# Token tiles of v, with their ones column, at a stride of 192 bytes instead of 130

## The chip, the cores and the metric

The kernel runs on one core of one Trainium2 chip. The metric is the device time of one execution in microseconds (us).

## The reference

Sparse attention (4 batches, 8 heads, 768 tokens, head dimension 64) followed by a gated feed-forward layer:

```python
scores = scale * np.matmul(q, k.transpose(0, 1, 3, 2))
scores = np.where(mask, scores, -1000000000.0)
attn = np.exp(scores - np.max(scores, axis=-1, keepdims=True))
attn = attn / (np.sum(attn, axis=-1, keepdims=True) + 1e-09)
o = np.matmul(attn, v)
# ... o is laid out as x: 3072 tokens x 512
gate = 1.0 / (1.0 + np.exp(-(x @ w_gate)))
out = (gate * (x @ w_val)) @ w_out
```

The argument touches only `attn @ v` and the row sum of `attn`.

## The kernel before

The tokens are cut into six tiles of 128. For each head and token tile, v stands in SBUF as 64 columns in fp16, followed by one column of ones. One matmul thus gives both the product and, in column 65, the sum that divides it. The layout is dense: 65 elements of 2 bytes, so a tile begins 130 bytes after the one before.

```python
vex = [sing.tile([128, H, NT, D + 1], f16, name=f"vex{r}") for r in range(2)]
for r in range(2):
    nc.vector.memset(vex[r][:, :, :, D : D + 1], 1.0)
# ...
def go(eng):                                  # VectorE: v of one batch and two heads
    nc.vector.tensor_copy(
        vex[b % 2][:, 2 * p : 2 * p + 2, :, 0:D],
        v16[:, 2 * p : 2 * p + 2, :, :],
    )
# ...
def pv(self, s):                              # TensorE: called with s = 0 and s = 1
    acc = spare[self.bank.slot][:, 0 : 4 * (D + 1)]
    self.acc = acc.rearrange("a (s h d) -> a s h d", s=2, h=2)
    for a in range(2):
        for t in range(NT):
            nc.tensor.matmul(
                self.acc[:, s, a, :],
                self.steps[t // 2].pt[:, a, t % 2, s * 128 : (s + 1) * 128],
                vex[self.b % 2][:, 2 * self.p + a, t, :],
                start=(t == 0),
                stop=(t == NT - 1),
            )
```

The two calls make 24 matmuls in a row: twice (s) over two heads (a) and six token tiles (t). There are 48 such groups, 1152 matmuls. Each has a weight load of its own (the probabilities, 128 columns), and v is the operand that streams: the profile of before lists 1152 loads of `pt`, 128x128, and 1152 matmuls with 128x65 of `vex`. The order of all work comes from a planner with fixed costs, so it does not depend on the layout.

The softmax here doesn't subtract the row's maximum and nothing guards it: scores larger than these inputs give would overflow.

Of the kernel before, what the change touches and what calls it, by code (L numbers as in the profile page):

```python
# [13 lines left out]
f16 = mybir.dt.float16  # L14
# [6 lines left out]
B, H, S, D = 4, 8, 768, 64  # L21
BLK = 32
NB = S // BLK
NT = S // 128
# [10 lines left out]
XB, PB, VB = 4, 5, 5  # L35
BIG = 1024.0
FFN_LAG = 3



# [83 lines left out]
def kernel(  # L124
# [18 lines left out]
            name=nc.get_next_instruction_name(), act_func_set_id=_set_id  # L143
# [17 lines left out]
    sing = ctx.enter_context(tc.tile_pool(name="sing", bufs=1))  # L161
# [17 lines left out]
    qp = sing.tile([128, NP, NT, 2, D], f16, name="qp")  # L179
    kp = sing.tile([128, NP, NT, 2, D], f16, name="kp")  # L180
    v16 = sing.tile([128, H, NT, D], f16)
    vex = [sing.tile([128, H, NT, D + 1], f16, name=f"vex{r}") for r in range(2)]
    qT = [sing.tile([128, NP, S], f16, name=f"qT{r}") for r in range(2)]
    kT = [sing.tile([128, NP, S], f16, name=f"kT{r}") for r in range(2)]

# [296 lines left out]
    class Pair:  # L482
# [9 lines left out]
        def pv(self, s):  # L492
# [4 lines that stand above are left out]
                    nc.tensor.matmul(  # L497
                        self.acc[:, s, a, :],
                        self.steps[t // 2].pt[:, a, t % 2, s * 128 : (s + 1) * 128],
                        vex[self.b % 2][:, 2 * self.p + a, t, :],  # L500
                        start=(t == 0),
                        stop=(t == NT - 1),
                    )
# [66 lines left out]
    def scores(run):  # L570


        def mm(eng):
            for pr, st in run:
                st.qk()

        deps = [
            x for pr, st in run for x in kdone[pr.b, pr.p] + qdone[pr.b, pr.p, pr.u]
        ]
        first = run[0][0].n == 0  # L580
        if first:
            deps.append(t_bias)
        a = plan.add(
            [(PE, 0.1 + (0.44 if first else 0.22) * len(run))],
            mm,
            deps,
            take=[st.bank for pr, st in run],
        )
        for pr, st in run:
            read["qk", pr.b, pr.p] = [a]  # L590
            i = NP * pr.n + pr.p - VB
            old = [used["P"][i]] if i >= 0 else []
            e = plan.add([(ACT, 0.98)], st.exp, [a] + old, free=[st.bank])
            if first:
                pr.products.append(e)
                continue
            pr.products.append(plan.add([(DVE, 0.66)], st.mul, [e] + masks[st.j, st.u]))
# [239 lines left out]
    for n in range(1, len(units)):  # L837
# [5 lines left out]
        for sl in range(6):  # L843
# [4 lines left out]
            else:  # L848
                scores(run)
            part = parts.popleft() if n > 1 or sl >= FFN_LAG else []  # L850
            for i, fn in enumerate(part):
# [50 lines left out]
```

## Time and profile before

| | before |
|---|---|
| time, median (range of runs) | 298.56 us (298.49 to 298.87) |
| span of the profiled run | 297.6 us (that run took 299.34 us) |
| TensorE busy | 289.9 us, 97% |
| ScalarE, VectorE busy | 205.1 us, 191.0 us |
| value product (line 497) | 1152 matmuls; 0.77 us on the chain for 24 |

The prediction shows the lines themselves. Below, the *distance* of two matmuls is the time from the start of one to the start of the next. It is read from the pieces of the chain (duration divided by count) or from the records' start times, never from the mean duration of one matmul (at line 497 that is 194 ns, while one starts every 32 ns). The *chain* is the sequence of work that ended last, followed back from the end.

### The profile page before, as it was taken

What the parts mean: (1) busy time and instruction counts of PE and PEld (TensorE: products, weight loads), DVE (VectorE), ACT (ScalarE), POOL (GpSimd) and SP (SyncE); (2) the same over time, 40 slices, a digit from 0 to 9 for tenths busy, and PEclk for the clock granted to TensorE, in tenths of its full rate; (3) what the DMA queues carried; (4) which work ended last, traced back from release to release, by engine and by line L of the source; (5) the groups of instructions that cost most, each with busy time, mean ns of one, the idle gap of its engine ahead of it and who ended that gap; (6) DMA issues with size and microseconds to landing.
All of it is one profiled execution on the core that took longest, in us unless ns stands there. A gap on an engine that the chain in (4) does not pass through costs nothing.

```text
span 297.6 us, 7862 instructions
## 1 busy us (share of the span) xinstructions
PE 289.9 (97%) x3302; PEld 206.2 (69%) x3302; DVE 191.0 (64%) x439; ACT 205.1 (69%) x323; POOL 48.5 (16%) x65
## 2 busy tenths in 40 slices
PE   7998999999999999999999999999999999999994
PEld 2655785786786786786776786686687687687771
DVE  3588877875675677676576577577477477475240
ACT  2689977677677677677777776777777677672331
POOL 8944100197000000097100000000000000000000
PEclk9999999999999999999999999999999999999999
DMA  7999999999900200999940202920201200201101
GB/s 109 185 201 203 206 204 205 212 174 149 193 12 9 90 13 10 173 177 133 179 70 18 83 11 56 203 64 20 79 11 20 79 11 20 78 15 20 70 2 71
DMA packets 74540, 28.55 MB, mean 96 GB/s; under 512 B 57352, under 2 KB 71560, under 8 KB 74504
## 3 DMA queue, kind: packets, MB, share of 16 engines
q0 software_dynamic: 40400, 14.16, 43.7%
q1 hardware_dynamic: 33924, 13.75, 20.5%
q8 instruction: 26, 0.43, 0.6%
q10 hardware_dynamic: 180, 0.13, 0.1%
q14 instruction: 10, 0.08, 0.1%
HBM read 28.55 MB, written 6.29 MB: 117 GB/s over the span
## 4 chain that ended last, share of the span: by engine, by line
PE 92%; ACT 2%; DMA 2%; DVE 1%; POOL 1%; issue 0%; ACTq 0%; POOLq 0%
PE m L617 44%; PE m L657 22%; PE s L459 12%; PE m L497 12%; DMA k<-in_k_dram 2%; ACT pt L469 2%; PE s L451 1%; PE m L382 1%; PE m L347 1%; ACT qT L232 0%; PE m L518 0%; POOL k L188 0%; ACT kT L232 0%; POOL q L188 0%; POOL v L188 0%
## 5 line engine op out<-in xcount | busy, mean ns | idle before, releaser
L469 ACT ACTIVATE pt<-s 128x1024 f16<-128x1024 f32 x144 | 139.9, 1023 | 9.5 <-PE s L459 9.4
L475 DVE TENSOR_TENSOR pt<-pt,mask 128x1024 f16<-128x1024 f16 x132 | 91.0, 690 | 52.0 <-ACT pt L469 51.9
L628 ACT ACTIVATE th<-m 128x256 f32<-128x256 f32 x144 | 54.3, 388 | 48.0 <-PE m L617 47.2
L617 PE MATMUL m<-xT,wg 128*128 128x256 f16 x576 | 86.8, 273 | 0.3 <-DVE x L509 0.3
L617 PE MATMUL m<-xT,wv 128*128 128x256 f16 x576 | 86.4, 273 | 0.0
L633 DVE SCALAR_TENSOR_TENSOR ht<-th,m 128x256 f16<-128x256 f32 x144 | 56.6, 417 | 20.8 <-ACT th L628 20.5
L657 PE MATMUL m<-wo,ht 128*128 128x512 f16 x288 | 66.1, 380 | 0.0
L617 PEld LDWEIGHTS <-wv 128*128 128x128 f16 x576 | 56.3, 98 | 6.5
L617 PEld LDWEIGHTS <-wg 128*128 128x128 f16 x576 | 50.5, 98 | 14.8 <-issue 9.7
L657 PEld LDWEIGHTS <-ht 128*128 128x128 f16 x288 | 26.5, 98 | 32.8 <-issue 4.2
L459 PE MATMUL s<-qT,kT 64*128 64x256 f16 x576 | 48.0, 275 | 1.1 <-ACT pt L469 0.8
L497 PEld LDWEIGHTS <-pt 128*128 128x128 f16 x1152 | 43.3, 98 | 3.8 <-issue 0.6
L497 PE MATMUL m<-vex,pt 128*128 128x65 f16 x1152 | 45.1, 194 | 0.0
L459 PEld LDWEIGHTS <-kT 64*128 64x128 f16 x576 | 23.0, 95 | 17.4 <-issue 13.6
L694 ACT ACTIVATE ysb<-m 128x512 f32<-128x512 f32 x23 | 13.7, 597 | 23.7 <-PE m L657 23.7
L740 POOL DMA_DIRECT2D kp<-in_k_dram x16 | 13.0, 820 | 80.8 <-DMA kT<-kp 53.7
L509 DVE TENSOR_TENSOR x<-m,rz 128x256 f16<-128x256 f32 x48 | 20.4, 424 | 1.7
L507 DVE RECIPROCAL rz<-m 128x4 f32<-128x4 f32 x48 | 8.7, 181 | 15.1 <-PE m L497 15.1
L740 POOL DMA_DIRECT2D qp<-in_q_dram x16 | 13.0, 819 | 2.2 <-DMA kp<-in_k_dram 1.9
L451 PE MATMUL s<-bias,e 64*128 64x256 f16 x48 | 7.2, 319 | 0.2 <-ACT pt L469 0.2
L382 PE MATMUL m<-ident,pr 128*128 128x128 f16 x48 | 5.2, 264 | 0.8 <-DVE pr L373 0.4
L234 DVE CAST mask<-m 128x512 f16<-128x512 f32 x9 | 5.7, 681 | 0.4 <-PE m L347 0.4
(45 smaller groups left out, 67.2 us busy)
## 6 DMA issues: line engine op xcount, KB each, us to landing
out_dram<-ysb SPq DMA_DIRECT2D x23, 256.0 KB, 2.0
v<-in_v_dram POOLq DMA_DIRECT2D x3, 768.0 KB, 11.1
wg<-in_moe_w_gate_dram POOLq DMA_DIRECT2D x4, 384.0 KB, 12.8
wv<-in_moe_w_val_dram POOLq DMA_DIRECT2D x4, 384.0 KB, 14.0
wo<-in_moe_w_out_dram POOLq DMA_DIRECT2D x3, 512.0 KB, 16.9
kp<-in_k_dram POOLq DMA_DIRECT2D x16, 96.0 KB, 5.8
qp<-in_q_dram POOLq DMA_DIRECT2D x16, 96.0 KB, 4.9
k<-in_k_dram POOLq DMA_DIRECT2D x4, 192.0 KB, 5.8
```

The source lines that it names most:

```text
L451: nc.tensor.matmul(score[self.bank.slot][:, o // D, i, :], e64[o : o + D, t * 128 : (t + 1) * 128], bias[o : o + D, :], start=True, stop=F ...
L459: nc.tensor.matmul(score[self.bank.slot][:, o // D, i, :], kT[b % 2][o : o + D, p, t * 128 : (t + 1) * 128], qT[b % 2][o : o + D, p, u * U ...
L469: nc.scalar.activation(self.pt, score[self.bank.slot], AF.Exp, bias=0.0, scale=SCALE)
L475: nc.vector.tensor_tensor(self.pt, self.pt, m.unsqueeze(1).broadcast_to([128, 2, 2, UQ]), op=ALU.mult,)
L497: nc.tensor.matmul(self.acc[:, s, a, :], self.steps[t // 2].pt[:, a, t % 2, s * 128 : (s + 1) * 128], vex[self.b % 2][:, 2 * self.p + a, t ...
L509: nc.vector.tensor_tensor(self.x16, self.acc[:, :, :, 0:D], rz.broadcast_to([128, 2, 2, D]), op=ALU.mult,)
L617: nc.tensor.matmul(pg[:, i, :], w[:, c, f * 128 : (f + 1) * 128], xTs[self.n][0][:, c, :], start=(c == 0), stop=(c == 3),)
L628: nc.scalar.activation(th, spare[bank.slot][:, 0:UQ], AF.Tanh, bias=0.0, scale=0.5)
L633: nc.vector.scalar_tensor_tensor(self.ht[:, f, :], in0=box[0], scalar=1.0, in1=spare[bank.slot][:, UQ : 2 * UQ], op0=ALU.add, op1=ALU.mult,)
L657: nc.tensor.matmul(spare[bank.slot], self.ht[:, f, s * 128 : (s + 1) * 128], wo[:, f, :], start=(f == 0), stop=(f == NF - 1),)
L694: nc.scalar.activation(ysb, spare[bank.slot], AF.Copy, bias=0.0, scale=0.5)
L740: nc.gpsimd.dma_start(dst[:, p, :, a, :], src[b, 2 * p + a].rearrange("(n t) d -> n t d", t=NT),)
```

## The change

Each token tile gets 96 elements (192 bytes) instead of 65, of which 65 are still written and read. The intent is that every tile starts on a round address and the streaming read becomes cheaper. It costs 5,952 bytes per partition.

```diff
+VW = 96
...
-    vex = [sing.tile([128, H, NT, D + 1], f16, name=f"vex{r}") for r in range(2)]
+    vex = [sing.tile([128, H, NT, VW], f16, name=f"vex{r}") for r in range(2)]
...
-                        vex[self.b % 2][:, 2 * self.p + a, t, :],
+                        vex[self.b % 2][:, 2 * self.p + a, t, 0 : D + 1],
```

## The prediction

A *line* here and below is 16 bytes of the array that begin at a multiple of 16. The grain of 16 is read from the trace of before: leaving out the first matmul of each half of a 24, those whose tile starts at an odd multiple of 16 bytes take 29.3 ns, those at an even one 29.2 ns (48 records each), and those at 8 bytes past a multiple of 16 take 32.4 ns (96 records). The four interleaved lines of rival 3 are a supposition that no trace shows.

> **What bounds the kernel now.** I read the page first, then the chain of work that ended last (as a summary and stretch by stretch), then the busy time by stretch, then the groups of TensorE and VectorE by line and form.
>
> The page: one engine is full and the others are not.
>
> ```profile
> PE 289.9 (97%) x3302; PEld 206.2 (69%) x3302; DVE 191.0 (64%) x439; ACT 205.1 (69%) x323; POOL 48.5 (16%) x65
> PE 92%; ACT 2%; DMA 2%; DVE 1%; POOL 1%; issue 0%; ACTq 0%; POOLq 0%
> PE m L617 44%; PE m L657 22%; PE s L459 12%; PE m L497 12%; DMA k<-in_k_dram 2%; ACT pt L469 2%; PE s L451 1%; PE m L382 1%; PE m L347 1%; ACT qT L232 0%; PE m L518 0%; POOL k L188 0%; ACT kT L232 0%; POOL q L188 0%; POOL v L188 0%
> ```
>
> TensorE is 92% of the chain, and line 497, the product of the probabilities with v and its ones column, the only reader of the array that changes its stride, is 12% of the span, some 36 us. "Busy" alone would not do, since matmuls overlap. So the stretches:
>
> ```profile
> 12.00:40.00 28.00, 26.45 (x374) 18.66 (x371) 22.52 (x55) 24.95 (x34) 10.03 (x13) 1.00 1.31 203
> 40.00:80.00 40.00, 40.00 (x480) 28.70 (x478) 28.45 (x68) 29.31 (x47) 13.86 (x17) 1.00 1.54 193
> 120.00:160.00 40.00, 40.00 (x495) 30.26 (x493) 27.11 (x60) 29.12 (x47) 13.89 (x17) 1.00 1.30 136
> 240.00:260.00 20.00, 20.00 (x234) 14.25 (x233) 12.65 (x27) 15.04 (x24) 0.00 (x0) 1.00 0.11 35
> ```
>
> The columns are the length, then busy time and count of PE, weight loads, DVE, ACT and POOL, then the granted clock. From 40 us to about 280 us PE never stops, at full clock, and ACT and DVE are busy some 70% of the time: every nanosecond of PE time there is a nanosecond of the kernel. From 12 to 40 us PE stands still for 1.55 us and the chain runs through ACT and mask work about half the time, so a gain there counts about half.
>
> What one matmul costs on that chain is read from the pieces of the chain in order of time, because a group's "mean ns of one" is latency, not pace:
>
> ```profile
> 108.51 0.77 PE m L497 x24
> 109.28 1.75 PE m L617 x16
> 111.03 0.54 PE s L459 x8
> ...
> 118.85 2.70 PE m L657 x12
> 121.55 0.77 PE m L497 x24
> ```
>
> 0.77 us for 24 matmuls of line 497 is 32 ns each; 1.75 us for 16 of 256 columns is 109 ns; and line 657, with 512 columns, starts one every 216 ns by the records' start times. A straight line through the last two, (216 - 109.2) / 256, is 0.417 ns for a column and 2.5 ns for a matmul. For the 65 columns of line 497 it gives 27.1 + 2.5 = 29.6 ns. The observed 32.25 ns (mean distance of starts inside the 24s, over all of them) is **2.65 ns too much**, and that excess is what the change can be after.
>
> [...] the copy into the odd-stride array takes about what a copy of the same size into an even layout takes.
>
> ```profile
> L428 DVE COPY vex<-v 128x768 f16<-128x768 f16 x16 | 5.1, 364 | 1.0 <-DMA v<-in_v_dram 1.0
> L408 DVE COPY qp<-q 128x768 f16<-128x768 f16 x4 | 1.2, 354 | 0.0
> L497 PE MATMUL m<-vex,pt 128*128 128x65 f16 x1152 | 45.1, 194 | 0.0
> L497 PEld LDWEIGHTS <-pt 128*128 128x128 f16 x1152 | 43.3, 98 | 3.8 <-issue 0.6
> ```
>
> **Where the 2.65 ns sit.** I sorted the start distances of line 497 by which token tile each matmul reads. With a stride of 130 bytes, tile number r of the array starts at 130 r bytes; this is a multiple of 16 for r a multiple of 8. A matmul on such a tile holds the array 29.3 ns (96 records, not counting the first of each half of a 24); the ordinary others hold it 32.8 ns (911 records). The first matmul of the second half of each 24, which jumps back six or more tiles, is also fast, and this whether its tile starts on a line (29.6 ns, 24 records) or in the middle of one (29.2 ns, 24 records). So the bare alignment is not the whole rule. One rule fits all: a matmul is slow when its first 16-byte line is the one that the matmul before has just read the end of. Consecutive tiles at 130 bytes touch, so they share a line unless the next starts exactly on one; after the jump nothing is shared. That is my reading, not something the profile states. At 192 bytes the row of 130 ends in the ninth line of twelve, and no two tiles share a line; they all start on a line too, so the alignment reading predicts the same.
>
> **The change part by part.**
> - *Matmuls*: same 1152, same 65 columns, same order (the schedule is built from fixed costs, which the diff leaves alone). If all run at 29.6 ns, a 24 takes 710 ns instead of 24 x 32.25 = 774: 64 ns less. 1008 matmuls (42 groups) lie after 40 us, all on the chain: 42 x 64 = 2.7 us. The 144 between 12 and 40 us (6 groups) save 0.38 us, of which half counts: 0.2 us. Sum **2.9 us**, from 298.56 to about 295.7.
> - *Copies into the array*: 16 of 364 ns, on DVE, with slack; perhaps 10 ns less or more each, off the chain. Nothing.
> - *The two fills of the ones column*: 98 ns each at the start, still 48 elements. Nothing.
> - *Memory*: 48 tiles x 62 bytes more, twice: 5,952 bytes per partition. Later arrays move by that, 93 x 64 bytes, so they keep their position within a line. No transfer from memory touches the array. Nothing.
> - *Next bound*: with 2.7 us less PE time, ACT and DVE stay near 70%, so no other engine takes over.
>
> **The rivals.**
> 1. *The stall is given back in part.* After a fast matmul the next one is slower than usual: two in a row starting with a fast one take 62.7 ns, two ordinary ones 64.9. So a clean matmul saves 2.2 ns net, not 3.5. If that is a real limit behind (such as the pace of weight loads), 20 matmuls of each 24 win about 2.2 ns: 43 ns x 45 groups, 1.9 us, 296.6 us. Against it: the straight line says 29.6 for a free array.
> 2. *Weight loads set the pace.* Each matmul of line 497 has its own load of 128 columns, so both have the same mean distance. If loads cost 32 ns, nothing is won: 298.5 us. Against it: single distances of 29 ns occur exactly where the tile read is different, while the loads there are no different.
> 3. *It is a bank, not a line.* Should the stall come when two reads follow in the same one of four interleaved lines, the new layout keeps it: from the ninth line of a tile to the first of the next are four lines. Then the fast ones are lost too, at some 2.2 ns for each of 4 in a 24: 0.4 us more, 298.9 us. Nothing in the profile speaks for four rather than for the line itself, but nothing excludes it.
> 4. *More than 2% won.* This would take over 6 us, that is over 5 ns for each of 1152 matmuls, or 27 ns per matmul with no fixed part. The straight line excludes it.
>
> **Range and chances.** I give the full gain about 60%, the partial one 20%, no gain or a slight loss 17%, something else 3%. The runs of before scatter by 0.4 us. The centre is 295.8; a range of 294.9 to 298.0 holds the first two and their surroundings. All of them lie within 2%: faster by over 2% 0.02, within 0.97, slower 0.01.
>
> **What would show each step.** Right: the chain's pieces of line 497 fall from 0.77 us to about 0.71 per 24, start distances are 29 to 30 ns for every tile, without a pattern of eight, busy time of line 497 falls by about 3 us, all other lines keep their pace, and PE stays full from 40 to 280 us. The partial rival shows 0.73; rivals 2 and 3 show 0.77 or more, rival 3 without any 29 ns inside a head. Wrong in another way: 0.71 and yet no shorter span, with new idle time of PE waiting for ACT's exponentials. What would make the prediction wrong most easily is that the first fast matmul is only early and the stream as a whole is paced by something else.

## The result, and the profile after

The changed kernel took 296.35 us in the median (296.30 to 297.39, 4 runs) against 298.56 us. The ratio is 0.9932, 95% interval 0.9909 to 0.9955. Ratios here are the mean time of one kernel's fast runs over that of the other's of the same rounds, so not quite the ratio of the medians. Executions in which one die ran at a lower clock are left out of the means.

First the page of the kernel after: busy time by engine, and the shares of the chain by line. Every line number is one higher, since the diff adds a line.

```profile
PE 287.0 (97%) x3302; PEld 203.8 (69%) x3302; DVE 191.2 (65%) x439; ACT 205.2 (70%) x323; POOL 48.3 (16%) x65
PE m L618 44%; PE m L658 22%; PE s L460 13%; PE m L498 11%; ACT pt L470 2%; DMA k<-in_k_dram 1%; PE m L383 1%; PE s L452 1%; ACT kT L233 1%; PE m L348 1%; ACT qT L233 0%; PE m L519 0%; DVE pr L374 0%; DVE pt L476 0%; DVE kT L235 0%
```

TensorE lost 2.9 us of matmul time; VectorE, ScalarE and GpSimd changed by 0.2 us at most. The value product went from 12% to 11% of a shorter span. Next, two of the same stretches of busy time (length, then PE, weight loads, VectorE, ScalarE and POOL, then the granted clock, DMA share and GB/s):

```profile
40.00:80.00 40.00, 40.00 (x468) 28.28 (x466) 29.05 (x70) 28.87 (x48) 13.87 (x17) 1.00 1.57 189
120.00:160.00 40.00, 40.00 (x493) 29.90 (x490) 27.24 (x61) 29.88 (x49) 13.88 (x17) 1.00 1.14 129
```

TensorE is still full, so no wait took the place of the time saved. The pieces of the chain (start, duration, what) name the place:

```profile
106.72 0.73 PE m L498 x24
107.45 1.75 PE m L618 x16
109.20 0.54 PE s L460 x8
...
116.98 2.70 PE m L658 x12
119.68 0.73 PE m L498 x24
```

A group of 24 value products takes 0.73 us instead of 0.77; the feed-forward matmuls keep 1.75 us for 16 and 2.70 us for 12, the scores 0.54 us for 8. The groups of the copy into the array and of the value product (line, form, count, busy us, mean ns) show the rest:

```profile
L429 DVE COPY vex<-v 128x768 f16<-128x768 f16 x16 | 5.0, 352 | 0.4 <-DMA v<-in_v_dram 0.4
L498 PEld LDWEIGHTS <-pt 128*128 128x128 f16 x1152 | 41.3, 97 | 3.8 <-issue 0.6
L498 PE MATMUL m<-vex,pt 128*128 128x65 f16 x1152 | 43.0, 193 | 0.0
```

The copy took 352 ns instead of 364, but 373 and 369 ns in the two later profiles of the same changed kernel, so this is scatter. The matmul's own duration hardly moved (194 to 193 ns); only its busy time fell, from 45.1 to 43.0 us.

**Where the spans differ.** Both traces list the same 3302 matmuls in the same order, so I can compare the start of the n-th in each. From the 301st to the 3151st, which is from about 30 us to just after the last value product, the kernel before takes 241.64 us and the changed one 239.83 us: **1.81 us less**, gained evenly. The profiled spans differ by 3.04 us, and the other 1.23 us had already arisen by the 301st matmul. Of these, 1.10 us were there when the first value product (the 66th matmul) began, at 12.16 us instead of 13.26. That part is no effect of the layout, since nothing had yet read the array; in three profiles of the changed kernel the first value product starts at 12.16, 13.29 and 12.43 us. From there to the seventh group, at about 40 us, the kernel before takes 26.94 us and the changed one 26.76, 26.75 and 26.74, so 0.17 to 0.20 us are gained early. The stretch after the 301st is 239.83 us in all three. I therefore use this **steady stretch** below; it repeats to within 1 ns where the median time moves by 0.8 us.

### The profile page after: what moved, and what is told of

Same layout as the page of the kernel before. It is cut to its first block, busy times and chain, and to the rows that moved or that the text cites. A ratio compares the mean times of both kernels' runs of the same rounds, so it can differ in the third digit from the quotient of the medians.

```text
span 294.5 us, 7862 instructions
## 1 busy us (share of the span) xinstructions
PE 287.0 (97%) x3302; PEld 203.8 (69%) x3302; DVE 191.2 (65%) x439; ACT 205.2 (70%) x323; POOL 48.3 (16%) x65
## 4 chain that ended last, share of the span: by engine, by line
PE 93%; ACT 3%; DVE 1%; DMA 1%; issue 0%; ACTq 0%; POOLq 0%
PE m L618 44%; PE m L658 22%; PE s L460 13%; PE m L498 11%; ACT pt L470 2%; DMA k<-in_k_dram 1%; PE m L383 1%; PE s L452 1%; ACT kT L233 1%; PE m L348 1%; ACT qT L233 0%; PE m L519 0%; DVE pr L374 0%; DVE pt L476 0%; DVE kT L235 0%
## 5 line engine op out<-in xcount | busy, mean ns | idle before, releaser
L460 PE MATMUL s<-qT,kT 64*128 64x256 f16 x576 | 47.3, 273 | 1.1 <-ACT pt L470 0.8
L498 PEld LDWEIGHTS <-pt 128*128 128x128 f16 x1152 | 41.3, 97 | 3.8 <-issue 0.6
L498 PE MATMUL m<-vex,pt 128*128 128x65 f16 x1152 | 43.0, 193 | 0.0
```

The lines of the kernel that those rows point to most:

```text
L460: nc.tensor.matmul(score[self.bank.slot][:, o // D, i, :], kT[b % 2][o : o + D, p, t * 128 : (t + 1) * 128], qT[b % 2][o : o + D, p, u * U ...
L498: nc.tensor.matmul(self.acc[:, s, a, :], self.steps[t // 2].pt[:, a, t % 2, s * 128 : (s + 1) * 128], vex[self.b % 2][:, 2 * self.p + a, t ...
```

## The experiments

The question is why 65 columns at 130 bytes are slower. The prediction's theory: a matmul is slow if its first 16-byte line is the one the matmul before has just read the end of. Rivals: the tile must start on a line (alignment); neighbouring lines collide by bank; weight loads set the pace. The edits are shown in part: where the column count or the place of the ones changes, the fills, the copy into the array and the width of the accumulator were changed with it. The main figures are also in the table at the end of this section.

**The change again, twice.** No edit; it is the yardstick in the rounds of the others.

> The changed kernel as it is, once more, on the chip and in the rounds of the next three, as their yardstick. Expected 296.3 us, 2.2 us under the kernel before, with pieces of 0.73 us for 24 matmuls of the value product in the chain; no theory differs here.

Measured: 297.18 us against 298.34, ratio 0.9957 (0.9933 to 0.9982), and 0.73 us per 24. The medians differ by 1.2 us, not by the 2.2 expected.

> The changed kernel again, in the rounds of the 66-column one, as its yardstick and for a closer interval of the change itself: a ratio of 0.993 to 0.995 to the kernel before, 0.73 us per 24.

Measured: 296.83 us against 298.47, ratio 0.9955 (0.9938 to 0.9972), and 0.73 us per 24. The medians of the three sittings, 296.35, 297.18 and 296.83 us, show the scatter of the start; the gain itself is in each of them.

**Stride 144, the least with whole lines.**

```diff
-VW = 96
+VW = 72
```

> Stride 144 bytes: nine 16-byte lines, the least stride at which every tile of 130 bytes starts on a line and no two tiles share one; successive tiles start 16 bytes further within 64. Shared-line theory: as at 192, 0.73 us per 24, about 296.3 us. Alignment to 16 bytes: the same. Alignment to 32 or 64 bytes (the reason one would pick 192 for): half or three quarters of the tiles slow again, some 0.75 to 0.76 us per 24, about 297.3 to 298. A bank theory in which neighbouring lines collide: no gain, 298.5.

Measured: 296.91 us, ratio 0.9947 (0.9925 to 0.9969); 0.73 us per 24, and a steady stretch of 239.84 us, as with 192. So neither 32- nor 64-byte alignment made a difference here, and neighbouring lines did not collide. The size of a line shows as well: with lines of 32 bytes half of the neighbours at stride 144 would share one and be slow, and with lines of 8 bytes the tiles of the old layout that start on 8 but not on 16 bytes would be fast, yet they take 32.4 ns (96 records), against 29.3 on a multiple of 16 (96 records). The same gain costs 1,344 bytes per partition instead of 5,952.

**Stride 146: no line shared, seven of eight tiles off a line start.**

```diff
-VW = 96
+VW = 73
```

> Stride 146 bytes: a gap of 16 bytes follows each tile, so no two tiles share a line, but only one tile in eight starts on one. Shared-line theory: fast as at 192, 0.73 us per 24, about 296.3 us. Alignment theory (a tile must start on a 16-byte line): slow as before, 0.77 us per 24, about 298.5 us, with 29 ns only at each eighth tile.

Measured: 296.53 us, ratio 0.9936 (0.9918 to 0.9953). Two pieces of its chain:

```profile
106.73 0.73 PE m L498 x24
107.46 1.75 PE m L618 x16
```

The unaligned tiles are as fast as the aligned ones, 0.73 us per 24: the alignment rival falls. The steady stretch is 239.91 us, 0.08 us over that of 192, so a start inside a line cost next to nothing here.

**The old layout in another order.** Stride 130 stays; the six tiles are accumulated in the order 1 3 5 0 2 4, and no matmul follows on its neighbour.

```diff
-                for t in range(NT):
+                for i, t in enumerate((1, 3, 5, 0, 2, 4)):
...
-                        start=(t == 0),
-                        stop=(t == NT - 1),
+                        start=(i == 0),
+                        stop=(i == NT - 1),
```

> The kernel before with its stride of 130 bytes; only the order in which the six token tiles are accumulated is changed, from 0 1 2 3 4 5 to 1 3 5 0 2 4, so that no matmul follows on the neighbour of its tile. The results stay right. Shared-line theory: 0.73 us per 24 and about 296.4 us without any change of layout. Alignment theory: nothing changes, 0.77 us per 24 and 298.5 us.

Measured, with right results: the chain of this kernel, with the line number of before,

```profile
108.24 0.74 PE m L497 x24
112.25 0.73 PE m L497 x24
```

and a steady stretch of 240.01 us, 1.62 of the 1.81 us, without touching a byte of the layout. The median, 297.66 us (ratio 0.9960, 0.9930 to 0.9989), misses the 296.4 us expected. In the profiled run (297.98 us) this is the start, where the granted clock, the column before the last two, was low:

```profile
0.00:12.00 12.00, 8.57 (x57) 4.10 (x57) 5.62 (x20) 4.50 (x5) 10.83 (x19) 0.81 0.98 140
12.00:40.00 28.00, 26.45 (x370) 18.87 (x367) 22.40 (x55) 24.58 (x34) 9.84 (x13) 0.96 1.31 203
```

Its 301st matmul began at 30.46 us. The fastest of the four runs took 296.48 us.

**Aligned, but touching.** A stride of 128 bytes with 65 columns read: every tile starts on a line, and its 65th element is the first of the next tile. The ones stand in that element, so one dimension of v is lost; the result is wrong.

```diff
-    vex = [sing.tile([128, H, NT, D + 1], f16, name=f"vex{r}") for r in range(2)]
+    vex = [sing.tile([128, H * NT * D + D], f16, name=f"vex{r}") for r in range(2)]
...
-                        vex[self.b % 2][:, 2 * self.p + a, t, :],
+                        vex[self.b % 2][
+                            :, ((2 * self.p + a) * NT + t) * D : ((2 * self.p + a) * NT + t) * D + D + 1
+                        ],
```

> Wrong results on purpose (one of the 64 dimensions is left out, sums stay right). Stride 128 bytes with 65 columns read: every tile starts exactly on a 16-byte line, and the last element of a tile is the first of the next, so all neighbours share a line. Alignment theory: fast, 0.73 us per 24, 296.4 us. Shared-line theory: slow at every matmul but the two jumps, also at the tiles that were fast in the kernel before: 22 x 32.8 + 2 x 29.3 ns, so 0.78 us per 24, and 298.6 us or a little more.

Measured: 298.61 us against 298.36, ratio 1.0011 (0.9994 to 1.0028). Its chain (the edit moves the value product to line 499):

```profile
100.39 0.78 PE m L499 x24
...
107.70 0.77 PE m L499 x24
```

The gain is gone although every tile is aligned; the steady stretch is 241.77 us, that of before (241.64). The distances from start to start show it one by one. They are from the records, in ns: medians over the ten groups of the first head pair after 40 us, in order of place.

```
stride 130     29 35 33 32 33 32 33 32 29 34 32 33 30 32 33 32 32 32 32 32 30 33 32
stride 128     29 35 33 32 33 32 33 32 33 32 33 32 29 32 32 32 32 32 32 32 32 32 32
stride 192     29 35 29 29 29 29 35 29 29 29 29 35 29 29 29 29 35 29 29 29 29 35 29
```

At stride 130 the 9th and the 21st of this head pair start on a line of their own and are fast. At 128 these two are slow like all others, and only the first and the 13th, which come after a jump, are fast. At 192 all are fast except about every fifth, which takes 35 ns. That step is what remains of the excess over the prediction's straight line (0.417 ns for a column and 2.5 ns for a matmul): the mean is 30.43 ns, not 29.6.

**More and fewer columns.** The next runs look at that step. With 81 columns (the additional 16 are filled with ones, not with zeros as the expectation says; results right):

```diff
-                        vex[self.b % 2][:, 2 * self.p + a, t, 0 : D + 1],
+                        vex[self.b % 2][:, 2 * self.p + a, t, 0:81],
```

> The changed kernel with 81 columns read from each tile instead of 65 (16 columns of zeros more, results right). The straight line of 0.417 ns for a column and 2.5 ns for a matmul gives 36.25 ns. If the 35 ns steps that stay after the change at every fifth matmul come from a limit of about 30.4 ns for a pair of weight load and matmul, they vanish here: start distances 36 ns throughout, 0.87 us per 24. If they are an extra stall of some 6 ns at each fifth matmul, distances of 42 ns remain and it takes 0.90 us per 24.

With 49 columns (wrong):

```diff
-                        self.acc[:, s, a, :],
+                        self.acc[:, s, a, 16 : D + 1],
...
-                        vex[self.b % 2][:, 2 * self.p + a, t, 0 : D + 1],
+                        vex[self.b % 2][:, 2 * self.p + a, t, 16 : D + 1],
```

> Wrong results on purpose (16 dimensions are left out). The changed kernel with 49 columns instead of 65, each start still on a line. The straight line gives 22.9 ns and 0.55 us per 24. If the weight load of 128 columns (or the issue of the pair) sets a floor of 30.3 to 30.4 ns, the 24 stays at 0.73 us, with nearly all distances about 30 ns or a similar mix of 29 and 35. If the columns set the pace after the change and the steps of 35 ns are their own stall, the 24 falls to about 0.58 us.

A piece of the chain of each, 81 columns first:

```profile
102.59 0.89 PE m L498 x24
```

```profile
105.94 0.60 PE m L498 x24
```

At 81 columns the distances are 36 and, at every fifth, 42 ns (mean 37.10); the step stays although there is more time for the weight loads. At 49 columns a pair of load and matmul follows every 25.15 ns, so weight loads and issue set no floor of 30 ns here. That rival falls. 49 columns came near the second expectation (0.60 us per 24 for 0.58), with an even 25 ns and no step. The straight line says 22.9 ns, so something else may hold them there; no run looks for it. A step could be hidden by it.

**Stride and order together.** Stride 192 with the order 1 3 5 0 2 4.

> Stride 192 bytes and the order 1 3 5 0 2 4 together. Shared-line theory: both remove the same stall, so nothing adds up: 0.73 us per 24 as with either alone. If the order does something of its own to the weight loads, the 24 differs from 0.73 us.

Measured: 0.73 us per 24 and a steady stretch of 239.91 us, so nothing adds up. Both remove the same stall.

**64, 66 and 72 columns.** Does the step come of an odd count, or of a last line used in part? 64 columns fill eight lines (wrong: the ones replace a dimension), 72 fill nine (results right), and 66 is even but fills no line.

```diff
-                        vex[self.b % 2][:, 2 * self.p + a, t, 0 : D + 1],
+                        vex[self.b % 2][:, 2 * self.p + a, t, 0 : D + 2],    # 66; 0:D for 64; 0 : D + 8 for 72
```

> The changed kernel with 66 columns (a second column of ones, results right), so that the count is even and each product starts 264 bytes after the one before in its accumulator. Straight line: 30.0 ns. If the 35 ns step at each fifth matmul comes of the odd count or of the accumulator's odd start, it vanishes: distances of 30 ns, 0.72 us per 24, some 0.3 us less than the changed kernel. If not, 30 and 36 ns mixed, mean 30.8, 0.74 us per 24, some 0.4 us more than it.

> Wrong results on purpose (the ones take the place of one dimension). The changed kernel with 64 columns, eight whole lines, accumulators 256 bytes apart. Straight line: 29.2 ns. If the odd count or the half-used last line makes the step at each fifth matmul, it vanishes: 0.70 us per 24. If it is a stall of the stream whatever the count, the mean is some 30.0 ns and a 24 takes 0.72 us.

> The changed kernel with 72 columns, nine whole 16-byte lines (seven more columns of ones, results right). Straight line: 32.5 ns. If the step of some 6 ns at every fifth matmul comes of a last line of which only part is used (65 and 81 columns both use one element of it, and 64 columns, which show no step, fill theirs), there is no step here: 32 to 33 ns throughout, 0.78 us per 24. If it comes with any count over 64, the steps stay: mean 33.7 ns, 0.81 us per 24.

The chains of 64 and of 72 columns:

```profile
187.24 0.70 PE m L498 x24
```

```profile
188.62 0.78 PE m L498 x24
```

```
81 columns     36 42 36 36 36 36 42 36 36 36 36 42 36 36 36 36 42 36 36 36 36 42 36
72 columns     31 32 32 32 33 32 33 32 33 32 33 32 33 32 33 32 33 32 33 32 33 32 33
64 columns     28 29 29 30 29 29 29 29 29 30 29 29 29 29 29 30 29 29 29 29 29 30 29
```

With whole lines there is no step, also above 64 columns: 29.13 ns at 64 and 32.39 ns at 72, where the straight line says 29.2 and 32.5. So the step is not a matter of more than 64 columns here; it is there at 65 and 81, which both use one element of their last line. The 66-column run was to part odd counts from partial lines. Its profile fell into the slow state (granted clock 0.855), so its means cannot be compared, but its pattern can. In this run the lower clock shows as pauses: of its 256-column matmuls, most start either 109 to 110 or 135 to 139 ns apart. Between the pauses one group of the first head pair reads

```
66 columns     29 36 50 36 29 30 29 29 35 38 29 35 30 29 29 43 36 29 29 30 29 35 36
```

Of the run's 966 distances on the value product after 40 us, 584 are 29 or 30 ns, 243 are 35 or 36, and none lies from 31 to 34. Nowhere do five of 29 or 30 follow each other, just as with 65 columns, while with 64 they do so at 745 places. An even 30 ns, expected if the odd count or the accumulator's odd start made the step, is not there: **the step stays with an even count**. The five fast runs took 296.95 us in the median (ratio 0.9946, 0.9934 to 0.9958), the changed kernel 296.83 in those rounds; the scatter of the start hides differences of this size.

What is left is the last line used in part, as at 65, 66 and 81 columns, against whole lines at 64 and 72. This is not shown as the cause: the width of the accumulator that is written changes with the columns that are read, and no run parts the two.

| kernel | us per 24 on the chain | mean distance after 40 us, ns | steady stretch, us |
|---|---|---|---|
| before, stride 130 | 0.77 | 32.20 | 241.64 |
| stride 192 (the change) | 0.73 | 30.43 | 239.83 |
| stride 144 | 0.73 | 30.44 | 239.84 |
| stride 146 | 0.73 | 30.52 | 239.91 |
| stride 130, order 1 3 5 0 2 4 | 0.73 to 0.74 | 30.65 | 240.01 |
| stride 128, touching (wrong) | 0.77 to 0.78 | 32.33 | 241.77 |
| 192, other order | 0.73 | 30.43 | 239.91 |
| 192, 49 columns (wrong) | 0.60 | 25.15 | 234.31 |
| 192, 64 columns (wrong) | 0.70 | 29.13 | 238.61 |
| 192, 72 columns | 0.78 | 32.39 | 242.05 |
| 192, 81 columns | 0.89 | 37.10 | 246.70 |

None of the runs is clearly better than the changed kernel. Stride 144 equals it with less memory.

## Why the prediction was right or wrong

- **The bound**: right. TensorE stayed full (40.00 of 40.00 us in each stretch shown after), and the time saved after the start is in the value product alone (0.77 to 0.73 us per 24, the other pieces unchanged).
- **The mechanism**: right, and now shown. The stall follows the shared line, not the start: it is gone without alignment (stride 146, steady stretch 239.91 us), gone but for a tenth without a new layout (other order, 240.01 us), and present with full alignment (stride 128, 241.77 us), where before has 241.64 and the change 239.83. What happens inside the memory or its reader is not shown by any run.
- **The size**: the term that failed is "If all run at 29.6 ns, a 24 takes 710 ns instead of 24 x 32.25 = 774: 64 ns less." All neighbours are free now, but the mean distance is 30.43 ns, because a step to 35 ns comes at about every fifth matmul. A 24 saves 24 x (32.20 - 30.43) = 42 ns, and the steady stretch, which begins some 10 us earlier, 1.81 us instead of the 2.7 us of that term. The time, 296.35 us, lies in the range, 0.55 us above the centre, but part of the 2.2 us between the medians is scatter of the start: by the traces the layout won 0.17 to 0.20 us before about 40 us and 1.9 to 2.0 us in all, of the 2.9 expected.
- **Rival 1**, the gain given back in part, is what came, by the prediction's own sign (0.73 us per 24, not 0.71), though it had been given only 20%. Its size was right (43 ns per 24, 1.9 us), in part by luck. It rests on 64.9 ns for two ordinary matmuls, but that mean, by the records, includes pairs whose second is a fast one; without these it is 65.4 against 62.9, 2.6 ns saved and not 2.2. Its suggested reason did not hold: a pair of load and matmul runs at 25.15 ns with 49 columns. The step is there at 65, 66 and 81 columns and not at 64 and 72; why it comes about every fifth time is open.
- **Rival 2** (weight loads) and **rival 3** (banks of four lines) fell, the first by 49 columns (25.15 ns), the second by the gain at 192 (1.81 us of the steady stretch), where four lines lie between the end of one tile and the start of the next.
- **The 0.2 us of the early stretch**: measured as 0.17 to 0.20, but by two errors that offset each other. The chain there was to run about half through ACT and mask work; in fact the lines of TensorE are 68% of it. And a 24 saves 42 ns, not 64: 6 x 42 x 0.68 = 0.17 us.
- **Copies, fills, memory, next bound**: right; no effect on the copy is shown (352 to 373 ns after, 364 before).

## What to carry to other kernels

When the engine is full, compare the distance of starts with a straight line through other shapes of the same kernel; the excess (here 2.65 ns of 32.25), sorted by address and place in the sequence, led to the cause before any run. In this kernel, streaming operands of 65 columns that lie side by side and are read one after the other took 32.33 ns each where they share a 16-byte line (stride 128) and 30.43 where they do not (stride 192), all starts aligned. A gap did it (1.81 us less in the steady stretch), and another order did nearly the same for nothing (1.62 us less). A pattern "aligned ones are fast" can have another cause, and a case that is fast without being aligned (here the jump, 29.2 ns in 24 records) is what separates the two.
